# The output product of the last two batches as a two-by-two block product with seven products

## The chip, the cores and the metric

The kernel runs on one core of one Trainium2 chip. The metric is device time in microseconds (us). The matrix engine is TensorE (PE in the rows), its weight loads are listed apart (PEld); VectorE is DVE, ScalarE is ACT, SyncE (SP) issues all transfers.

## What is computed

Attention with a soft cap on its scores for four batches of twelve heads, 448 positions of width 64; the heads laid side by side (768 columns) go through a two-layer block: w_in (768 x 2048), a sigmoid gate, w_out (2048 x 768).

```python
scores = scale * np.matmul(q, k.transpose(0, 1, 3, 2))
scores = cap * np.tanh(scores / cap)
scores = scores - np.max(scores, axis=-1, keepdims=True)
attn = np.exp(scores)
attn = attn / (np.sum(attn, axis=-1, keepdims=True) + 1e-09)
x = np.matmul(attn, v)                          # then (batch, seq, heads * 64)
h = x @ w_in
g = h * (1.0 / (1.0 + np.exp(-1.702 * h)))
return g @ w_out
```

## The kernel before

The work is one batch (448 columns) at a time, numbered 0 to 3, and is written transposed: features on the 128 partitions, positions along the free dimension.

*Attention* goes by units of two heads, six units to a batch. From unit 8 on, all of batches 2 and 3, operands are pairs of 16-bit tiles (a rounded part and the rest). A unit makes four groups of scores into the two double banks of `ps_s` (line 494); ScalarE takes the tanh and the exponential and rounds p, VectorE forms the rest of p and adds the exponentials into `ta` for the sums. There are five p tiles (482), four to a unit. Then come the sums (`ps_sm`) and the products with v (`ps_pa`), one bank each. The sums go through DRAM and come back broadcast as `rb` (two tiles, 486); VectorE multiplies, and `xh` and `xl` are written. For each of the six units there is one tile of xh and one of xl (498), which serve all batches in turn: batch 3's can be written only when batch 2's have been read for the last time.

*h* of a batch (`h_unit`, 727) is 16 chunks of 128 features, `fc`: 6 x 3 matmuls of 128 x 448 into one of two banks (`ps_m`, 409), three because both operands are pairs and the product of the two rests is left out. ScalarE takes the tanh, VectorE multiplies, and `gh`, `gl` are written into one buffer (499) that every batch uses. *The output product* (`o_unit`, 743) is six chunks `dc` of 128 rows, each 16 x 3 matmuls into one bank, one evacuation on ScalarE and one transfer out.

*Order.* The main loop (817) lists attention unit by unit and, in between (`slot`, 785, by the amounts in `BUDGET`), steps of `moe_h` and `moe_o` (768, 778), batch after batch. Each step becomes an operation with its inputs, outputs and an estimated cost. `Plan.schedule` (312) then puts the operations of every engine into a fixed order: up to 20 times it plays them forward, each engine taking the operation that can start first (priority decides ties), and backward, for the latest starts that become the next priorities; the shortest order is written out. Tiles of a ring are given out in the order in which they were asked for. The waits between engines follow from the tiles.

At the end `verdict` (849) forms a flag from column sums kept in `fin` (454) and from a few maxima; only if it is set does a general path run as well (352).

Of the kernel before, what the change touches and what calls it, by code (L numbers as in the profile page):

```python
# [28 lines left out]
DEC_ON = ("AV", "AV")  # L29
EV_ON = ("AV", "AV")  # L30
PASSES = 20
IDLE_MIN, IDLE_STEP = 0.5, 0.06


# [59 lines left out]
class Plan:  # L94
# [263 lines left out]
def fast_path(ctx, tc, flag, q, k, qx, kx, v, cap, w_in, w_out, out):  # L358
# [3 lines left out]
    plan = Plan(tc)  # L362
    B, NP, _, S = q.shape
# [3 lines left out]
    P = 128  # L367
    NC = 8
    NCC = DM // P
    NFC = DFF // P  # L370
# [17 lines left out]
    def ring(shape, dt, name, n, pool=sb):  # L388
        return plan.ring([pool.tile(shape, dt, name=f"{name}{i}") for i in range(n)])
# [19 lines left out]
    ps_m = ring([P, 512], F32, "m", 2, ps)  # L409
# [6 lines left out]
    for i, s in enumerate((1.0, QS * QS)):  # L416
        t = sb.tile([P, 1], F32, name=f"tsc{i}")
# [21 lines left out]
    W0, W1 = 512, 384  # L439
    wi_t = [sb.tile([P, NCC, DFF], F16, name=nm) for nm in ("wi_h", "wi_l")]  # L440
    wo_s = sb.tile([P, 4 * NFC * W1], F16, name="wo")
    wo_t = [[wo_s[:, (2 * c + i) * NFC * W1:(2 * c + i + 1) * NFC * W1].rearrange("p (r w) -> p r w", w=W1) for i in range(2)] for c in range(2)]

    wseq = [(0, r, n, c, W0) for c in range(0, DFF, W0) for r, n in (W_FIRST if c == 0 else ((0, 2), (2, 2), (4, 2)))]
    wseq += [(1, r, WO_ROWS[c], c * W1, W1) for c in range(2) for r in range(0, NFC, WO_ROWS[c])]
    pieces = {}
    wi, wo = {}, {}
# [3 lines left out]
        for i in range(n):  # L451
            (wo if m else wi)[r + i, c] = [x[:, i] for x in both]

    fin = sb.tile([P, len([z for z in wseq if z[0]]) + B * NFC], F32, name="fin")
    fins, fcol = columns(fin, 1)


# [28 lines left out]
    rb_r = ring([P, S], F32, "rb", 2)  # L486
    pu_r = ring([P, S], F32, "pu", 2)
# [255 lines left out]
    def o_unit(b, dc):  # L743
# [11 lines left out]
        plan.scaled(ob, po[:, :S], OS, psum=True)  # L755
        plan.dma([(out[dc * P:(dc + 1) * P, b * S:(b + 1) * S], ob)], P * S * 4e-6)

    ready = set()
    last = {}
    pend = []  # L760
    budget = [0.0]

    def need(m, col):

        while done[0] < len(wseq) and (wseq[done[0]][0] < m or (wseq[done[0]][0] == m and wseq[done[0]][3] <= col)):
            decode_w()

    def moe_h(b):
        while b not in ready:
            yield None  # L770
        for fc in range(NFC):
            need(0, fc * P)
            h_unit(b, fc)
            if b == B - 1 and fc == NFC - 1:
                last["g"] = gs[fc][0]
            yield 3.5

    def moe_o(b):
# [271 lines left out]
```

## Time and profile before

| | |
|---|---|
| three timed runs | 631.75, 632.32, 632.40 us; median 632.32 |
| the profiled execution | 631.68 us, span 629.5 us, granted clock 0.998 |
| TensorE busy | 619.0 us, 98% |
| VectorE, ScalarE busy | 385.8 us (61%), 392.9 us (62%) |
| matmuls h <- x, w_in | 1152 |
| matmuls out <- g, w_out | 1152 |

A busy time is the sum of the listed durations with overlap counted once; matmuls are pipelined, so that what one costs in a stream is read from the time of a long run of them and its count. The page cuts the span into 40 slices; each digit is a busy share in tenths:

```profile
PE   7999999999999999999999999999999999999996
DVE  5688998999788866686664376687664113331000
ACT  6999896799699757778647458779647113331000
```

Attention of the last unit ends near slice 31 of 40; behind it lie h and the output product of batch 3.

### The profile page before, as it was taken

Reading aid. Unit: us, or ns where it says so; the run is one execution under the profiler, and the core shown is the slowest. Engines: PE = TensorE matmul, PEld = TensorE weight load, DVE = VectorE, ACT = ScalarE, POOL = GpSimd, SP = SyncE. Lnnn points to the kernel's source line nnn. Section 1 sums busy time; section 2 is a strip of 40 time slices with the busy share of each in tenths; the row PEclk is TensorE's granted clock in tenths of the full one; section 3 lists DMA queues with packets and bytes.
Section 4 is the critical chain, followed back from the end, with each engine's and each line's share of the span. In section 5 each row is a group of like instructions: output and inputs, shape, how many; then the busy total and the mean of one; then the engine's idle time right before and its main releaser. Section 6 shows DMA issues by size and latency. Waiting matters only on the chain.

```text
span 629.5 us, 9528 instructions
## 1 busy us (share of the span) xinstructions
PE 619.0 (98%) x3743; PEld 296.4 (47%) x3743; DVE 385.8 (61%) x684; ACT 392.9 (62%) x536; POOL 0.2 (0%) x4
## 2 busy tenths in 40 slices
PE   7999999999999999999999999999999999999996
PEld 3343344444444445445445545445445555555553
DVE  5688998999788866686664376687664113331000
ACT  6999896799699757778647458779647113331000
POOL 0000000000000000000000000000000000000000
PEclk9999999999999999999999999999999999999999
DMA  8977651541666821211321321200111100000000
GB/s 301 408 231 195 229 179 51 191 133 56 167 164 191 264 90 32 77 46 46 105 101 35 106 73 48 80 13 18 26 38 44 31 30 1 0 1 17 29 16 34
DMA packets 36340, 61.29 MB, mean 97 GB/s; under 512 B 13928, under 2 KB 21952, under 8 KB 36288
## 3 DMA queue, kind: packets, MB, share of 16 engines
q1 hardware_dynamic: 36288, 60.61, 30.6%
q8 instruction: 31, 0.51, 0.3%
q14 instruction: 21, 0.17, 0.1%
HBM read 54.93 MB, written 5.66 MB: 96 GB/s over the span
## 4 chain that ended last, share of the span: by engine, by line
PE 93%; ACT 2%; DMA 2%; DVE 1%; issue 1%; SPq 0%; ACTq 0%; DVEq 0%
PE m L198 70%; PE s L198 10%; PE pa L198 9%; PE sm L198 3%; DMA wo<-in_moe_w_in_dram 1%; ACT p L155 1%; ACT t L155 1%; ACT wi_h L179 1%; DMA wo<-in_q_dram 1%; ACT wo L179 0%; DVE wi_l L163 0%; DVE wo L163 0%; ACT stg L179 0%; SPq L204 0%; DVE wo L186 0%
## 5 line engine op out<-in xcount | busy, mean ns | idle before, releaser
L198 PE MATMUL m<-gh,wo 128*128 128x448 f16 x768 | 216.2, 353 | 0.0
L198 PEld LDWEIGHTS <-wo 128*128 128x128 f16 x1152 | 110.7, 98 | 107.9 <-issue 7.0
L198 PE MATMUL m<-xh,wi_h 128*128 128x448 f16 x384 | 135.6, 353 | 0.0
L198 PE MATMUL m<-xl,wi_h 128*128 128x448 f16 x384 | 135.4, 353 | 0.0
L198 PE MATMUL m<-gl,wo 128*128 128x448 f16 x384 | 135.4, 353 | 0.0
L198 PE MATMUL m<-xh,wi_l 128*128 128x448 f16 x384 | 135.4, 352 | 0.0
L155 ACT ACTIVATE t<-s,tsc 128x896 f32<-128x896 f32 x96 | 87.0, 907 | 46.5 <-PE s L198 46.4
L198 PEld LDWEIGHTS <-wi_h 128*128 128x128 f16 x768 | 72.8, 98 | 78.7 <-issue 13.7
L163 DVE SCALAR_TENSOR_TENSOR f<-f,m 128x448 f32<-128x448 f32 x64 | 39.5, 618 | 53.1 <-ACT f L155 52.9
L155 ACT ACTIVATE f<-m 128x448 f32<-128x448 f32 x64 | 34.6, 541 | 59.0 <-PE m L198 57.8
L179 ACT ACTIVATE f<-m 128x448 f32<-128x448 f32 x23 | 12.4, 539 | 84.0 <-PE m L198 75.8
L163 DVE TENSOR_TENSOR ta<-ta,t 128x896 f32<-128x896 f32 (+1 forms) x48 | 41.0, 855 | 32.1 <-ACT t L155 30.9
L198 PEld LDWEIGHTS <-wi_l 128*128 128x128 f16 x384 | 37.6, 98 | 35.1
L163 DVE SCALAR_TENSOR_TENSOR wo<-wo 128x1024 int32<-128x1024 int32 (+3 forms) x50 | 51.9, 1053 | 3.2 <-ACT wo L179 2.6
L155 ACT ACTIVATE t<-t,lnb,capt 128x896 f32<-128x896 f32 (+1 forms) x52 | 52.9, 1016 | 1.4
L163 DVE SCALAR_TENSOR_TENSOR gl<-f,gh 128x448 f16<-128x448 f32 x64 | 39.6, 622 | 16.9 <-ACT gh L179 16.3
L163 DVE TENSOR_TENSOR p<-t,p 128x896 f16<-128x896 f32 (+1 forms) x52 | 48.9, 942 | 1.2 <-ACT p L179 0.9
L198 PE MATMUL s<-qh,kk 128*128 128x448 f16 (+3 forms) x160 | 47.5, 401 | 0.0
L179 ACT ACTIVATE p<-t 128x896 f16<-128x896 f32 (+1 forms) x52 | 43.4, 834 | 1.4
L198 PE MATMUL s<-ql,kk 128*128 128x448 f16 (+1 forms) x128 | 39.5, 352 | 0.0
L179 ACT ACTIVATE gh<-f 128x448 f16<-128x448 f32 x51 | 29.1, 570 | 13.7 <-DVE f L163 13.7
L198 PE MATMUL pa<-p,vh 128*64 128x448 f16 x256 | 35.4, 357 | 0.0
(94 smaller groups left out, 545.6 us busy)
## 6 DMA issues: line engine op xcount, KB each, us to landing
wo<-in_moe_w_in_dram SPq DMA_DIRECT2D x24, 512.0 KB
stg<-in_kx_dram SPq DMA_DIRECT2D x16, 448.0 KB
stg<-in_qx_dram SPq DMA_DIRECT2D x16, 448.0 KB
stg<-in_moe_w_out_dram SPq DMA_DIRECT2D x16, 384.0 KB
wo<-in_moe_w_out_dram SPq DMA_DIRECT2D x16, 384.0 KB
out_dram<-f SPq DMA_DIRECT2D x24, 224.0 KB
rb<-rd SPq DMA_DIRECT2D x44, 112.0 KB
vd<-in_v_dram SPq DMA_DIRECT2D x18, 256.0 KB
```

The costliest lines, as they stand in the source:

```text
L155: self.nc.scalar.activation(real(out), real(in_), func, scale=real(scale), **b)
L163: getattr(self.nc.vector, name)(out=real(out), **{k: real(x) for k, x in ins.items()}, **kw, **a)
L179: self.nc.scalar.activation(real(out), real(in_), AF.Copy, scale=1.0 if f is None else f, **b)
L198: self.nc.tensor.matmul(real(o), real(w), real(x), start=a, stop=z)
```

## The change

The output product of batches 2 and 3 together is read as one product of two-by-two blocks. The blocks of w_out are halves of the 2048 features (`j`, 8 chunks each) by halves of the 768 outputs (`i`, three chunks each); the blocks of g are halves of the features by batch. Winograd's form of Strassen's product needs four sums T of blocks of g, four of w_out, seven block products and a few additions behind them. For each of three pairs `d` of output chunks (`d` and `d + 3`) there are seven products of 8 x 3 matmuls, in place of 4 x 16 x 3.

- `difference` replaces the upper right block of w_out by the difference of the upper two, for eight rows, listed after batch 1's output product.
- `h_pair` computes batch 3's h for two chunks, i and i + 8, at a time, and never writes batch 3's g: it forms T1 to T3 and two more operands (`tw`), each split into a pair of 16-bit tiles, from both batches' g. They go to tiles that attention has done with, `tw` to columns of w_in that have been used, in four rows of 112 columns. Its banks are all six of `ps_m` and `ps_s`, and it waits until those are done with.
- `seven_first` (two products, and batch 2's first outputs) runs for d = 0 behind batch 2's h, listed within batch 3's attention; for d = 1, 2 behind batch 3's h.
- `seven_rest` (five products, three outputs) follows; `seven_a` forms three sums of w_out's blocks for a d beforehand, in the space of x and of w_in.
- The x tiles become slices of one tile; `fin` has other columns; the verdict is listed at the end.

```diff
+SPLIT_ON = "A"
+EARLY_FIRST = 1
...
-    x_r = [tuple(ring([P, S], F16, f"{nm}{p}_", 1) for nm in ("xh", "xl")) for p in range(NP)]
+    x_s = sb.tile([P, 2 * NP * S], F16, name="x")
+    x_r = [tuple(plan.ring([x_s[:, (2 * p + i) * S:(2 * p + i + 1) * S]]) for i in range(2)) for p in range(NP)]
...
+    tw = {(k, i): [plan.fixed(t[:, 0:4, (i + k * HF) * P:(i + k * HF) * P + QW]) for t in wi_t] for k in range(2) for i in range(HF)}
...
+    z_r = plan.ring([*ps_m["tiles"], *(t[:, i] for t in ps_s["tiles"] for i in range(2))])
+    e_r = plan.ring([*rb_r["tiles"], *pu_r["tiles"], *f_r["tiles"]])
...
+    def split_to(hi, lo, x, f=1.0, deps=((), ()), judge=False):
+        at(list(deps[0]), plan.scaled, hi, x, None if f == 1.0 else f, on=SPLIT_ON)
+        at(list(deps[1]), plan.stt, lo, x, f, hi, ALU.mult, ALU.subtract, accum_out=fcol() if judge else None)
+
+    def h_pair(i):
...
+        for fc in (i, i + HF):
+            ph = plan.turn(z_r)
...
+            plan.after = after(ps_m, ps_s)
...
+            t = plan.turn(e_r)
+            at(after(rb_r, pu_r, f_r), plan.act, t, ph[:, :S], AF.Tanh, scale=0.851 / HS)
+            plan.stt(t, t, 1.0, ph[:, :S], ALU.add, ALU.mult)
...
+        at(after(rb_r, pu_r, f_r), plan.stt, a, t1, GS, gs[i][0], ALU.mult, ALU.subtract)
+        plan.tt(a, a, gs[i][1], ALU.subtract)
+        tsplit(1, a)
+        plan.tt(t1, t2, t1, ALU.subtract)
+        tsplit(3, t1, GS)
+        split_to(*tw[1, i], four(t2), GS)
+        plan.stt(t2, t2, GS, a, ALU.mult, ALU.subtract)
+        tsplit(2, t2)
+        plan.tt(t2, t2, gs[HF + i][0], ALU.subtract)
+        plan.tt(t2, t2, gs[HF + i][1], ALU.subtract)
+        split_to(*tw[0, i], four(t2))
...
+    def difference(r):
...
+        u = plan.turn(pu_r)[:, :W1]
+        plan.tt(u, a, c, ALU.subtract)
+        plan.tt(u, u, al, ALU.add)
+        plan.tt(u, u, cl, ALU.subtract)
+        split_to(c, cl, u, judge=True)
+
+    def seven_a(d):
...
+        at(first + [x.buf for r in range(HF) for x in wo[r, W1]], plan.tt, u, q[1, 1][0], q[1, 0][0], ALU.subtract)
+        plan.tt(u, u, q[1, 1][1], ALU.add)
+        plan.tt(u, u, q[1, 0][1], ALU.subtract)
+        put(1, u)
+        at(first, plan.tt, w, u, q[0, 0][0], ALU.add)
+        plan.tt(w, w, q[0, 0][1], ALU.add)
+        put(0, w)
+        plan.tt(u, q[0, 1][0], u, ALU.subtract)
+        plan.tt(u, u, q[0, 1][1], ALU.add)
+        put(2, u)
...
+    def seven_first(d):
...
+        late = B - 1 in done_h
+        b1 = bank() if late else plan.turn(ps_m)
+        yield from product(b1, own(0, 0, d), gs[:HF])
+        part[d] = plan.turn(stg)[:, :S]
+        plan.scaled(part[d], b1[:, :S], OS, psum=True)
...
+    def seven_rest(d):
...
+        yield from product(p4, own(1, 1, d), [tw[0, r] for r in range(HF)])
+        seven_a(d)
...
+        yield from product(p7, own(1, 0, d), t_of(3))
...
+        yield from product(p6, s_of(1), t_of(2))
+        plan.stt(u2, p6[:, :S], OS, u2, ALU.mult, ALU.add)
...
+        yield from product(p5, s_of(0), t_of(1))
...
+        yield from product(p3, s_of(2), [tw[1, r] for r in range(HF)])
...
+    def moe_end():
+        while B - 1 not in ready:
+            yield None
+        for i in range(HF):
+            h_pair(i)
+            done_h.add(B - 1)
+            yield 7.0
+        yield from moe_last(range(EARLY_FIRST, HC))
+        for d in range(HC):
+            for _ in seven_rest(d):
+                yield 2.27
...
-            pend.append(moe_h(b))
-            pend.append(moe_o(b))
+            if b < B - 1:
+                pend.append(moe_h(b))
+                if b == B - 3:
+                    pend.append(moe_o(b))
+                    pend.append(moe_s3())
+                else:
+                    pend.append(moe_o(b) if b < B - 2 else moe_last(range(EARLY_FIRST)))
+            else:
+                pend.append(moe_end())
```

## Rows read from the trace of the kernel before

**Rows 1.** Page, part 1: busy time, share of span, instructions of each engine.

```profile
PE 619.0 (98%) x3743; PEld 296.4 (47%) x3743; DVE 385.8 (61%) x684; ACT 392.9 (62%) x536; POOL 0.2 (0%) x4
```

**Rows 2.** Windows, us: time, PE, PEld, DVE, ACT, POOL busy (count), clock, DMA, GB/s.

```profile
375.50:442.00 66.50, 66.50 (x388) 33.10 (x387) 47.81 (x86) 50.87 (x68) 0.00 (x0) 1.00 0.15 48
442.00:494.00 52.00, 52.00 (x326) 25.60 (x324) 27.46 (x42) 28.99 (x39) 0.00 (x0) 1.00 0.13 33
...
515.00:570.00 55.00, 55.00 (x293) 28.44 (x291) 19.38 (x46) 17.33 (x31) 0.00 (x0) 1.00 0.01 5
570.00:623.40 53.40, 53.40 (x284) 27.45 (x282) 1.62 (x9) 3.37 (x7) 0.00 (x0) 1.00 0.06 22
```

**Rows 3.** Chain of work that ended last, after 493 us: start, us, what.

```profile
493.74 129.50 PE m L198 x684
```

**Rows 4.** Groups by shape, whole run: engine operation shapes xcount | busy us, mean ns | idle.

```profile
L198 PE MATMUL m<-gh,wo 128*128 128x448 f16 x768 | 216.2, 353 | 0.0
...
L163 DVE SCALAR_TENSOR_TENSOR gl<-f,gh 128x448 f16<-128x448 f32 x64 | 39.6, 622 | 16.9 <-ACT gh L179 16.3
L163 DVE SCALAR_TENSOR_TENSOR f<-f,m 128x448 f32<-128x448 f32 x64 | 39.5, 618 | 53.1 <-ACT f L155 52.9
...
L179 ACT ACTIVATE gh<-f 128x448 f16<-128x448 f32 x51 | 29.1, 570 | 13.7 <-DVE f L163 13.7
...
L163 DVE SCALAR_TENSOR_TENSOR wi_l<-wo,wi_h 128x1024 f16<-128x1024 f32 x11 | 13.4, 1218 | 1.8 <-ACT wi_h L179 1.8
...
L163 DVE SCALAR_TENSOR_TENSOR wo<-stg,wo 128x384 f16<-128x384 f32 x16 | 8.8, 553 | 1.2 <-ACT wo L179 1.2
```

**Rows 5.** DVE timeline, three operations in a row: start, us, operation.

```profile
443.11 0.63 DVE L163 SCALAR_TENSOR_TENSOR xl<-rb,xh 128x448 f16<-128x448 f32 x1
443.65 0.61 DVE L163 SCALAR_TENSOR_TENSOR f<-f,m 128x448 f32<-128x448 f32 x1
444.19 0.62 DVE L163 SCALAR_TENSOR_TENSOR xl<-rb,xh 128x448 f16<-128x448 f32 x1
```

**Rows 6.** ACT timeline from the end of batch 2's h: start, us, operation.

```profile
442.12 0.56 ACT L179 ACTIVATE xh<-rb 128x448 f16<-128x448 f32 x1
...
445.64 0.53 ACT L155 ACTIVATE f<-m 128x448 f32<-128x448 f32 x1
...
448.59 1.01 ACT L155 ACTIVATE t<-s,tsc 128x896 f32<-128x896 f32 x1 [1.15 <-PE s L198]
449.63 1.13 ACT L155 ACTIVATE ta<-t,lnb,capt 128x896 f32<-128x896 f32 x1
450.79 0.95 ACT L179 ACTIVATE p<-ta 128x896 f16<-128x896 f32 x1
...
462.47 0.62 ACT L155 ACTIVATE t<-s,tsc 128x448 f32<-128x448 f32 x1
463.12 0.76 ACT L155 ACTIVATE t<-t,lnb,capt 128x448 f32<-128x448 f32 x1
463.91 0.58 ACT L179 ACTIVATE p<-t 128x448 f16<-128x448 f32 x1
```

**Rows 7.** Timeline of all engines around the last attention unit's end.

```profile
486.66 0.62 ACT L155 ACTIVATE t<-s,tsc 128x448 f32<-128x448 f32 x1
...
490.76 0.59 PE L198 MATMUL sm<-ta,ones 128*32 128x224 f32 x8
...
502.48 0.62 DVE L163 TENSOR_TENSOR rb<-pa,rb 128x448 f32<-128x448 f32 x1 [6.82 <-DMA rb<-rd]
...
505.23 0.54 ACT L179 ACTIVATE f<-m 128x448 f32<-128x448 f32 x1 [8.54 <-PE m L198]
...
505.67 0.57 ACT L179 ACTIVATE xh<-rb 128x448 f16<-128x448 f32 x1
...
506.28 0.62 DVE L163 SCALAR_TENSOR_TENSOR xl<-rb,xh 128x448 f16<-128x448 f32 x1 [3.18 <-ACT xh L179]
```

**Rows 8.** Windows again: the stretch after the last matmul (clock is third last).

```profile
626.00:629.50 3.50, 0.00 (x0) 0.00 (x0) 0.00 (x0) 0.00 (x0) 0.00 (x0) 0.70 0.04 12
```

More of the change, by code (lines that the diff above doesn't have):

```diff
@@ L452, in fast_path @@
             (wo if m else wi)[r + i, c] = [x[:, i] for x in both]
-    fin = sb.tile([P, len([z for z in wseq if z[0]]) + B * NFC], F32, name="fin")
+    fin = sb.tile([P, len([z for z in wseq if z[0]]) + (B - 1) * NFC + 2 + NFC // 2 + 3 * NCC // 2], F32, name="fin")
     fins, fcol = columns(fin, 1)
@@ L756, in o_unit, with after, blocks, flat16 @@
         plan.dma([(out[dc * P:(dc + 1) * P, b * S:(b + 1) * S], ob)], P * S * 4e-6)
+    HF, HC = NFC // 2, NCC // 2
+    QW = S // 4
+    def after(*rings):
+        return [b for r in rings for b in r["turns"]]
+    def blocks(t, n):
+        return [t[:, i * S:(i + 1) * S] for i in range(n)]
+    def flat16(t):
+        return t.rearrange("p a s -> p (a s)").bitcast(F16)
+    room_t = [(x, p_r) for t in p_t for x in blocks(t.rearrange("p w i s -> p (w i s)"), 4)]
+    room_t += [(x, r) for r in (t_r, ta_r) for t in r["tiles"] for x in blocks(flat16(t), 4)]
@@ new lines, in fast_path @@
+    room_t += [(x, r) for r in rings.values() for t in r["tiles"] for x in blocks(t.rearrange("p a s -> p (a s)"), 2)]
+    room_t += [(t[:, S:].bitcast(F16)[:, :S], stg) for t in stg_t]
+    t_at = {(k, i, w): (plan.fixed(x), r) for (k, i, w), (x, r) in zip(((k, i, w) for k in (1, 2, 3) for i in range(HF) for w in range(2)), room_t)}
+    tw = {(k, i): [plan.fixed(t[:, 0:4, (i + k * HF) * P:(i + k * HF) * P + QW]) for t in wi_t] for k in range(2) for i in range(HF)}
+    sw = {k: [plan.fixed(t[:, NCC - 2 + k // 2, k % 2 * HF * P:(k % 2 + 1) * HF * P].rearrange("p (r w) -> p r w", w=P)) for t in wi_t] for k in range(3)}
@@ new lines, in fast_path, with at @@
+    us = [plan.fixed(x_s[:, i * 2 * HF * P:(i + 1) * 2 * HF * P].bitcast(F32).rearrange("p (r w) -> p r w", w=P)) for i in range(2)]
+    z_r = plan.ring([*ps_m["tiles"], *(t[:, i] for t in ps_s["tiles"] for i in range(2))])
+    e_r = plan.ring([*rb_r["tiles"], *pu_r["tiles"], *f_r["tiles"]])
+    part = {}
+    done_h = set()
+    def at(deps, f, *a, **k):
+        plan.after = deps
+        f(*a, **k)
+        plan.after = []
+    def split_to(hi, lo, x, f=1.0, deps=((), ()), judge=False):
+        at(list(deps[0]), plan.scaled, hi, x, None if f == 1.0 else f, on=SPLIT_ON)
+        at(list(deps[1]), plan.stt, lo, x, f, hi, ALU.mult, ALU.subtract, accum_out=fcol() if judge else None)
@@ new lines, in quad, with put @@
+    def quad(i, j, d):
+        return [wo_t[i][w][:, j * HF:(j + 1) * HF, d * P:(d + 1) * P] for w in range(2)]
+    def difference(r):
+        (a, al), (c, cl) = wo[r, 0], wo[r, W1]
+        u = plan.turn(pu_r)[:, :W1]
[4 more added lines that the diff above has]
+    def seven_a(d):
+        q = {(i, j): [plan.fixed(x) for x in quad(i, j, d)] for i in range(2) for j in range(2)}
+        u, w = us
+        first = after(*(r for rs in x_r for r in rs)) if d == 0 else []
+        free = [x.buf for v in pieces.values() for x in v] if d == 0 else []
+        def put(k, x):
+            split_to(*sw[k], x, deps=(free, free), judge=True)
+        at(first + [x.buf for r in range(HF) for x in wo[r, W1]], plan.tt, u, q[1, 1][0], q[1, 0][0], ALU.subtract)
[8 more added lines that the diff above has]
+        put(2, u)
@@ new lines, in product @@
+    def product(out, lhs, mov):
+        for r in range(HF):
+            (wh, wl), (gh, gl) = lhs[r], mov[r]
+            o = out[:, :S]
+            if len(gh.shape) == 3:
+                o = o.rearrange("p (a w) -> p a w", w=QW)
+            plan.mm(3 * FULL, "full", [
+                (o, a, x, r == 0 and w == 0, r == HF - 1 and w == 2) for w, (a, x) in enumerate(((wh, gh), (wh, gl), (wl, gh)))
+            ])
+            plan.after = []
+            if r % 4 == 3 and r < HF - 1:
+                yield
@@ new lines, in own, with send, bank @@
+    def own(i, j, d):
+        return [[x[:, d * P:(d + 1) * P] for x in wo[j * HF + r, i * W1]] for r in range(HF)]
+    def send(ob, i, b, d):
+        dc = i * HC + d
+        plan.dma([(out[dc * P:(dc + 1) * P, b * S:(b + 1) * S], ob)], P * S * 4e-6)
+    def bank():
+        plan.after = after(ps_m, ps_s)
+        return plan.turn(z_r)
+    def seven_first(d):
[4 more added lines that the diff above has]
+        plan.scaled(part[d], b1[:, :S], OS, psum=True)
+        yield
+        b2 = bank() if late else plan.turn(ps_m)
+        yield from product(b2, own(0, 1, d), gs[HF:])
+        ob = plan.turn(e_r if late else f_r)
+        at(after(rb_r, pu_r, f_r) if late else [], plan.stt, ob, b2[:, :S], OS, part[d], ALU.mult, ALU.add)
+        send(ob, 0, B - 2, d)
@@ L773, in moe_h, with moe_s3, moe_last @@
             h_unit(b, fc)
-            if b == B - 1 and fc == NFC - 1:
-                last["g"] = gs[fc][0]
             yield 3.5
+    def moe_s3():
+        for r in range(HF):
+            difference(r)
+            yield 0.5
+    def moe_last(ds):
+        for d in ds:
+            for _ in seven_first(d):
+                yield 2.27
+            yield 2.27
+    def moe_end():
[8 more added lines that the diff above has]
+            for _ in seven_rest(d):
+                yield 2.27
+            yield 2.27
+            if d == HC - 1:
+                last["g"] = gs[NFC - 1][0]
     def moe_o(b):
```

45 lines of the change are left out of this document (added).

## The prediction

> **What bounds the kernel now.** I read the page's engine line first: TensorE is busy in 98% of the span, VectorE and ScalarE in 61% and 62% [rows 1]. The windows then show that this is an average over stages that differ: while batch 2's h runs, VectorE is busy 47.8 and ScalarE 50.9 of 66.5 us; in the stage of batch 3's h 19.4 and 17.3 of 55 us; in the last stage 1.6 and 3.4 of 53.4 us; TensorE fills all of them [rows 2]. So TensorE's amount of work sets the time now, and the other two have room at the end but much less where attention runs. The chain of waits says the same: its last long piece is one run of 684 matmuls in 129.50 us, 0.1893 us for each [rows 3]. Those are h of batch 3 (16 x 18 = 288), the output product of batch 3 (6 x 48 = 288) and 108 left over from batch 2's output product. The listed mean of 353 ns [rows 4] is a matmul's time through a pipeline, not its cost in a stream.
>
> **What is removed.** The output products of batches 2 and 3 are 2 x 6 x 16 x 3 = 576 matmuls. The change does seven block products for each of three column pairs, 7 x 8 x 3 x 3 = 504. 72 matmuls x 0.1893 = 13.6 us [rows 3]. All of these lie on the path. The profiled run took 631.68 us, 2.18 of it outside the span of 629.5 and 0.64 under the median of the three timed runs; without any loss the change would give 631.68 - 13.63 = 618.05.
>
> **What moves: the filler of the last attention.** Batch 2's output product is not only work; it covers. Of its 288 matmuls 180 (34.1 us) run while the last attention units wait on ScalarE and VectorE, and 108 (20.4 us) while the last unit's sums make their way through DRAM [rows 3]. In the new order only two of the seven products of the first column pair (48 matmuls, 9.1 us) can run there; the others need batch 3's g. The place begins where batch 2's h ends, since the x tiles have one buffer: the first two units of batch 3 get their xh written only at 442.12 and after, when the last h unit stops reading, and that unit's tanh starts at 445.64 [rows 6], so its last matmul ended near 445.6. From there to 493.74 TensorE worked 48.1 us, 34.1 of them filler, so attention's own share is 14.0 us, 3.0 of it the last unit's sums and products (490.76 to 493.74) [rows 3, 7]. In the new order it has 14.0 - 3.0 + 9.1 = 20.1 us of work until the scores of the last unit are evacuated (the h matmuls of batch 3 wait for all score banks). If the last tanh of the last unit starts by 445.6 + 20.1 = 465.7, nothing is lost; before, it starts at 486.66 [rows 7]. Every us beyond 465.7 is a us of idle TensorE.
>
> How early can it be? Unit 4's first tanh starts at 448.59. A unit's ScalarE work is three groups of 1.01 + 1.13 + 0.95 and one of 0.62 + 0.76 + 0.58, 11.2 us [rows 6]. Unit 4 whole, unit 5 without its last exponential and cast (11.2 - 1.34 = 9.9) and up to four short casts and evacuations of some 0.56 each, 2.2, make 23.3: the last tanh at 448.6 + 23.3 = 471.9 if ScalarE never waits and nothing goes to VectorE. Lower end: half of the casts go to VectorE (3.5 us less) and unit 4 starts when its keys allow, so 465.7 or earlier, loss 0. Upper end: the pace of before, in which unit 4 took 448.59 to 462.47 from first to last tanh [rows 6], 13.9 us, twice with a 2.5 us gap: 448.6 + 13.9 + 2.5 + 13.9 = 478.9, loss 13.2; with the very times of before 486.66, loss 21.0. I take 471.9, loss 6.2 us, since ScalarE's own rows carry it.
>
> After that tanh, sums, DRAM, product, xh and xl take until 506.90, 20.2 us, 2.5 of which xh stands behind an evacuation on ScalarE that waits for TensorE (rb is ready at 503.10, xh starts at 505.67) [rows 7]; so 17.7 to 20.2. TensorE has 3.0 us of that unit and, now that six banks may hold h, six units of 15 matmuls that don't need the last x: 90 x 0.1893 = 17.0. Together 20.0, so nothing more is lost there. Last x: 471.9 + 17.7 = 489.6.
>
> **What is added, and where it hides.** *Batch 3's h.* For each pair of fc VectorE has 13 operations of 128x448 in place of 4, ScalarE 6 in place of 4; TensorE needs 36 x 0.1893 = 6.8 us for a pair. VectorE's listed time is 0.62 [rows 4], but three such operations in a row start 0.54 apart [rows 5]: 13 x 0.54 = 7.0 us a pair, 56.2 for eight. ScalarE, 6 x 0.57 = 3.4, is covered. *The weight sums* of a column pair: seven subtractions or additions and three splits of 128x1024, at 1.22 listed and so 1.14 in a row (estimate: the same 0.08 less) [rows 4, 5]: 11.4 us of VectorE for each 22.7 us of TensorE (120 matmuls), hidden for the second and third pair, with six evacuations of 0.62 beside it. *The difference of w_out's halves*: 8 x 4 operations of 128x384 at 0.55 [rows 4], 17.7 us, wanted only after batch 3's h; VectorE is idle in 47% of the 52 us after batch 2's h [rows 2] and again while the last sums are under way, so I cost it at nothing. From the last x at 489.6, VectorE needs 56.2 + 11.4 + 1.1 (two evacuations), 68.7 us, until the last weight sum of the first column pair, and then TensorE has one product of that pair and two whole pairs, 264 matmuls or 50.0 us. That path ends at 608.3; TensorE's own at 623.24 - 13.63 + 6.2 = 615.8. So TensorE still carries the end, with 7.5 us to spare.
>
> The Trainium skill speaks against that cover: "VectorE: DVE Perf Modes", section "The DRAIN you can't avoid", has it that the next VectorE instruction does not start until the pipeline of the one before is empty. Here it starts 0.08 us before the listed end [rows 5], so the trace does not bear it out in full; taken at the listed 0.62 and 1.22 the sum would be 64.5 + 12.2 + 1.2 = 77.9 us, the path would end at 617.5 and the run 1.7 us later.
>
> *The moving operand in pieces.* Two of the seven products read T as four runs of 112 columns, a form that no row has. I take the price of the plain matmul; the upper end is the listed 353 ns for each of 2 x 72 matmuls [rows 4], 144 x 0.164 = 23.6 us; a gain is excluded, as the columns are the same number. *Queues*: SyncE issues the same 24 output transfers. The first part sum takes one of the four staging tiles through which keys and queries come; a load behind it would be late by one product, 24 x 0.1893 = 4.5 us, which belongs to A. *The end*: one VectorE operation in place of one ScalarE evacuation, under 0.1 us. *Small bubbles* where work of three engines is now tied closer: 1.0 us, between 0 and 4.
>
> Sum: 631.68 - 13.63 + 6.2 + 1.0 = 625.25.
>
> **Rivals.** A, the slower side: attention after batch 2's h does not speed up, because its pace was set by its own waits (score banks, one bank for the products, five p tiles) and not by the filler. Then the gain is eaten: the point is a last tanh at 465.7 + 13.6 = 479.3. With the times of before it is 618.05 + 21.0 + 1 = 640; with unit 5 right behind unit 4 at the old pace 618.05 + 13.2 + 1 = 632.3. For it: unit 4's first two groups lie 5.5 us apart where their ScalarE work is 3.1. Against it: VectorE and ScalarE are busy only 53% and 56% there [rows 2].
>
> B: VectorE becomes the bound in batch 3's h. It decides once VectorE has 7.5 us more than my 68.7. With listed durations it gives 627; with the 17.7 us of differences put off until there as well, 618.05 + 7.2 + 1.7 + 17.7 = 645. Half of that, some 635, is its middle.
>
> C: no loss at all, the attention is fast enough: 618 to 620.
>
> D: the clock. After the last matmul the granted clock is 0.70 over the last 3.5 us [rows 8], so it falls from 2.4 to 1.2 GHz when TensorE has stopped. The idle time that I forecast lies in pieces of a us or so between scores and products, so I leave it at nothing; in one piece it would slow the matmuls behind it. The Trainium skill, "TensorE: Matmul & The Clock Gate", section "Why this matters for your kernels", warns of such gaps between bursts; the trace agrees as far as its last stretch shows.
>
> E: the change does not do what it says: the flag sends the run into the general path as well, or the pieces of T cost as above (640).
>
> **How the numbers follow.** My forecast (620 to 630) 0.52, C 0.15, A 0.17 (half of it about 632, half slower), B 0.12 (a third of it under 630), D and E 0.04. Faster than 632.32 by over 0.2%, which is about what a measurement of this kernel can tell from no change (under 631.05): 0.52 + 0.15 + 0.04 = 0.71. Within: 0.09. Slower, over 633.6: 0.20, the rest of A and B, D and E. The range of 8 in 10 reaches from 618.0 (C) to 634.5, which takes in A's nearer end and the middle of B. Time: 625.3.
>
> **What would show it.** The matmuls of the output products should number 1080 in place of 1152. Right, if TensorE is idle for some 4 to 8 us between 445 and 472, in small pieces that wait for scores or p, and dense from there on; if the last unit's last tanh starts at 468 to 476; if in batch 3's h VectorE is busy over 85% and TensorE doesn't wait for it. Wrong, if TensorE waits on tiles written in batch 3's h (B), if its gaps lie in one piece with a lower clock (D), if matmuls on T's pieces start more than 0.19 us apart (E), or if the last tanh starts after 479 (A).

## The result and the profile after

The changed kernel takes 622.52 us (median of four runs, 621.96 to 623.3) where the kernel before took 632.36 in the same session (631.75 to 633.11): a ratio of 0.9845, 95% interval 0.9828 to 0.9862. That is 9.8 us less; the forecast was 625.3 with a range of 618.0 to 634.5. The time lies between the forecast and rival C. The profiled run took 622.88 us, 2.2 of them outside its span of 620.7, as before.

The page's engine line, in the form of [rows 1]:

```profile
PE 607.4 (98%) x3679; PEld 288.4 (46%) x3679; DVE 487.8 (79%) x845; ACT 408.6 (66%) x565; POOL 0.2 (0%) x4
```

VectorE has 102.0 us more to do than in [rows 1], ScalarE 15.7 more, and TensorE 11.6 less. Of TensorE's 3679 matmuls 85 are the small ones that the kernel puts into idle time at its start; before there were 77 of those among 3743. The rest went from 3666 to 3594, exactly the 72 that the change promises.

The windows (time, then busy time and count of PE, PEld, DVE, ACT and POOL, the granted clock, the DMA share, GB/s) for two of the stretches of [rows 2]:

```profile
375.50:442.00 66.50, 66.50 (x392) 31.84 (x387) 59.66 (x116) 52.55 (x74) 0.00 (x0) 1.00 0.14 42
515.00:570.00 55.00, 53.65 (x284) 27.58 (x282) 48.31 (x75) 17.76 (x30) 0.00 (x0) 1.00 0.03 9
```

TensorE is still full in the first. In the second it misses 1.35 us, and VectorE went from 19.4 us of the 55 to 48.3; in the 21 us ahead of it, from 494 to 515, VectorE is busy 20.7. So in batch 3's h VectorE now has hardly more room than TensorE. The chain of waits (start, us, what), where [rows 3] had one piece of 129.50 us:

```profile
429.86 3.41 PE m L200 x18
433.27 0.50 PE s L200 x4
433.77 3.51 PE m L200 x18
...
468.53 4.65 PE m L200 x24
473.17 3.41 PE s L200 x18
...
518.80 11.93 PE s L200 x63
530.75 0.55 ACT stg L181
531.35 8.67 PE s L200 x45
...
549.67 10.80 PE s L200 x57
560.49 0.64 DVE rb L165
561.17 6.97 PE s L200 x36
...
604.46 9.10 PE m L200 x48
613.58 0.62 DVE rb L165
```

It is still a chain of TensorE, with two short stops (an evacuation on ScalarE at 530.75, one on VectorE at 560.49). Where did the gain go? The span is 8.8 us shorter, the removed matmuls are worth 13.63, so 4.83 us are lost, and nearly all of them can be placed:

- 0.55 us up to the end of batch 2's h: of the matmuls on wi_l the 277th of 384, close to that end, starts at 438.86 and started at 438.31 (the order of the earlier stages changed a little). Six matmuls on v, some 0.6 us, that stood ahead of this point before now stand behind it.
- 1.35 us in the two stops, as idle time is listed, from the listed end of one matmul. From start to start they cost 1.68: the matmuls behind them start 0.99 and 1.07 us after the ones ahead, in place of 0.19.
- 0.88 us behind the last matmul: the span ended 6.26 us after it and now ends 7.14 after it.
- 2.05 us is what remains. 0.3 of it is the rest of the two stops, 0.6 the six matmuls on v, and 0.9 changes of the stationary tile's shape, which is listed ahead of the operand's size:

```profile
448.52 0.55 PE L200 MATMUL m<-x,wi_h 128*128 128x448 f16 x2
448.90 0.35 PE L200 MATMUL m<-x,wi_l 128*128 128x448 f16 x1
449.19 0.38 PE L200 MATMUL s<-qh,kk 128*64 128x448 f16 x2
```

A matmul ahead of such a change takes 0.28 to 0.29 us to the next start, where others of 128x448 take 0.19; so 18 matmuls behind a change take 3.51 us in the chain where others take 3.41. From the end of batch 2's h to the last matmul the changed kernel has 25 such changes and the kernel before 15: ten more at 0.094 us. All ten lie in the last attention; behind 494 us the chain goes from `m` to `s` and back without a change of shape, and 72 matmuls take 13.62 us as before. Some 0.2 us are left that no row explains.

How the attention's end came out (ScalarE's timeline: start, us, operation, and in brackets the idle time before it and what ended it):

```profile
441.88 1.01 ACT L157 ACTIVATE t<-s,tsc 128x896 f32<-128x896 f32 x1 [0.42 <-PE s L200]
...
461.50 0.62 ACT L157 ACTIVATE t<-s,tsc 128x448 f32<-128x448 f32 x1
...
479.67 0.58 ACT L181 ACTIVATE x<-rb 128x448 f16<-128x448 f32 x1 [6.89 <-DVE rb L165]
```

These answer to 448.59 of [rows 6] and to 486.66 and 505.67 of [rows 7]: unit 4 starts 6.7 us earlier than before, the last tanh of the last unit comes 25.2 us earlier, the last x 26.0. What stood ahead of unit 4's scores on TensorE, before (two lines) and after (two lines; the last is the end of batch 2's h):

```profile
447.44 0.35 PE L198 MATMUL m<-gh,wo 128*128 128x448 f16 x1
447.63 0.35 PE L198 MATMUL s<-qh,kk 128*128 128x448 f16 x1
...
440.91 0.36 PE L200 MATMUL s<-qh,kk 128*128 128x448 f16 x1
...
450.64 0.35 PE L200 MATMUL m<-x,wi_l 128*128 128x448 f16 x1
```

Before, the scores came behind all of batch 2's h and behind 12 matmuls of filler. After, they come ahead of the last 30 matmuls of batch 2's h.

### The profile page after: what moved, and what is told of

The parts are those of the page before. It is cut to its first block, busy times and chain, and to the rows that moved or that the text cites. A ratio compares the mean times of both kernels' runs of the same rounds, so it can differ in the third digit from the quotient of the medians.

```text
span 620.7 us, 9566 instructions
## 1 busy us (share of the span) xinstructions
PE 607.4 (98%) x3679; PEld 288.4 (46%) x3679; DVE 487.8 (79%) x845; ACT 408.6 (66%) x565; POOL 0.2 (0%) x4
## 4 chain that ended last, share of the span: by engine, by line
PE 93%; DMA 2%; DVE 2%; ACT 1%; issue 0%; SPq 0%; DVEq 0%; ACTq 0%
PE m L200 54%; PE s L200 26%; PE pa L200 10%; PE sm L200 4%; DVE wo L165 1%; DMA rb<-rd 1%; DMA rd<-rr 1%; DMA wo<-in_q_dram 1%; DVE wi_l L165 0%; ACT wo L181 0%; ACT t L157 0%; ACT p L157 0%; DVE rb L165 0%; SPq L206 0%; ACT wi_h L181 0%
## 5 line engine op out<-in xcount | busy, mean ns | idle before, releaser
L200 PE MATMUL m<-x,wi_h 128*128 128x448 f16 x648 | 175.8, 353 | 0.0
L200 PEld LDWEIGHTS <-wi_h 128*128 128x128 f16 x912 | 86.4, 98 | 93.4 <-issue 16.5
L200 PE MATMUL m<-gh,wo 128*128 128x448 f16 x432 | 124.4, 353 | 0.0
L200 PEld LDWEIGHTS <-wo 128*128 128x128 f16 x864 | 82.5, 98 | 82.7 <-issue 8.5
L200 PE MATMUL m<-x,wi_l 128*128 128x448 f16 x324 | 114.2, 352 | 0.0
L200 PE MATMUL m<-gl,wo 128*128 128x448 f16 x216 | 76.1, 352 | 0.0
L157 ACT ACTIVATE f<-m 128x448 f32<-128x448 f32 x49 | 26.4, 539 | 26.0 <-PE m L200 25.5
L165 DVE SCALAR_TENSOR_TENSOR gl<-f,gh 128x448 f16<-128x448 f32 x48 | 29.6, 622 | 4.6 <-ACT gh L181 4.0
L200 PE MATMUL s<-x,wi_h 128*128 128x448 f16 x120 | 32.5, 353 | 0.0
L200 PEld LDWEIGHTS <-kk 128*128 128x128 f16 (+1 forms) x256 | 20.5, 100 | 24.7 <-issue 8.4
```

Of the source, the lines that this page charges most:

```text
L157: self.nc.scalar.activation(real(out), real(in_), func, scale=real(scale), **b)
L165: getattr(self.nc.vector, name)(out=real(out), **{k: real(x) for k, x in ins.items()}, **kw, **a)
L200: self.nc.tensor.matmul(real(o), real(w), real(x), start=a, stop=z)
```

## The experiments

"Changed kernel" is the kernel of the diff; each experiment edits it, except one that edits the kernel before. Times are medians; a ratio is against the kernel before in the same session, with its 95% interval.

### 1. One product more in each column pair

```diff
         yield from product(p7, own(1, 0, d), t_of(3))
         yield
+        yield from product(p7, own(1, 0, d), t_of(3))
+        yield
         p6 = bank()
```

> The changed kernel with the eighth product given back: in each of the three column pairs the product of T3 is done twice in the same bank, the first time for nothing, 72 matmuls more. If TensorE carries the time through the last stages, it costs 72 x 0.1893 = 13.6 us, less what falls into TensorE's few waits: 634.5 to 636.5, slower than before by 0.4 to 0.6%. If VectorE bound batch 3's h and the stage behind it, much of the extra work would lie in TensorE's waits: 630 or less.

Measured: 637.55 us, ratio 1.0083 (1.0068 to 1.0098), 15.0 us over the changed kernel and 1 us past the range expected. The 72 matmuls cost all of their 13.6 us, and somewhat more than that: TensorE's waits for evacuations grew from 1.35 to 3.5 us, it may be because a bank stays taken longer; no run isolates that. So TensorE's work is on the path, one for one; nothing behind it absorbs a product. With seven plus one products the scheme is slower than the old eight.

### 2. No filler left beside the last attention

```diff
-EARLY_FIRST = 1
+EARLY_FIRST = 0
```

> EARLY_FIRST = 0: all of the seven-product scheme waits for batch 3's h, so 48 matmuls (9.1 us) leave the stretch of the last attention and the same number comes later. Theory: attention is now as fast as ScalarE allows, and what TensorE has there is what covers it; after the last score group TensorE had some 3 us of work beyond the arrival of the last x, so 9.1 - 3.4 = 5.7 us become idle: 627 to 629, with gaps of TensorE between 440 and 485. Rival: the last chunks of batch 2's h are spread wide enough to cover it: under 624.

Measured: 630.26 us, ratio 0.9969 (0.9956 to 0.9982), 7.7 us over the changed kernel and past both expectations. The filler's 9.1 us are worth most of their length there. TensorE's own rows in the place, and two windows, from the profiled run (631.95 us):

```profile
463.35 0.35 PE L200 MATMUL m<-x,wi_l 128*128 128x448 f16 x1
466.51 1.45 PE L200 MATMUL sm<-ta,ones 128*32 128x224 f32 x8 [2.82 <-DVE ta L165]
467.89 0.93 PE L200 MATMUL m<-x,wi_h 128*128 128x448 f16 x2
```

```profile
464.00:468.00 4.00, 1.40 (x9) 0.40 (x10) 3.83 (x7) 2.31 (x4) 0.00 (x0) 0.92 0.03 1
468.00:471.20 3.20, 3.20 (x10) 1.27 (x10) 2.58 (x6) 0.36 (x1) 0.00 (x0) 0.56 0.29 78
```

TensorE waits 2.82 us for VectorE's sum of ta, and then its matmuls start 0.37 us apart, not 0.19: the granted clock of the second window is 0.56 of full speed, so it has fallen from the higher of its two levels (2.4 GHz) to the lower (1.2) for most of it. By 471.2 it is back at 1.00. The chain has 3.22 us for nine matmuls that are 1.70 at full clock, so the fall cost 1.5 us in these nine. That is rival D's mechanism: it is not in the trace of the changed kernel, and it is there when the filler is gone. The rest is 2.7 us of waits for ScalarE at 454 and 456, the 2.82, and another 1.4 us of waits for evacuations in the last stage.

### 3. Two pairs of filler there

```diff
-EARLY_FIRST = 1
+EARLY_FIRST = 2
```

> Two column pairs of batch 2's first products (96 matmuls, 18.2 us) lie beside the last attention units, in place of one (48, 9.1 us). Theory: with one pair TensorE no longer waits there, so more filler buys nothing: 622 to 623.5 us. First rival: the bubbles of the stretch 440 to 494 come from work that is too thin, and more of it closes them: 620.5 to 621.5. Second rival: the filler stands in front of the last units' scores and moves the last x behind 484: over 625.

Measured: 625.72 us, ratio 0.9899 (0.9884 to 0.9914), 3.2 us over the changed kernel. The second rival's time, but only a part of its reason: the last x came 2.8 us later (483.05, where it was 480.28), and VectorE started batch 3's h at 488.20 in place of 484.29; but in experiment 5 it started at 489.05 and nothing was lost. TensorE has no gap at the last x. It waits later, from 490 on (engine, line, what it waited for, us in total, times, longest):

```profile
PE m L200 <- DVE stg L165: 0.9, 1, 0.9
PE s L200 <- DVE stg L165: 0.7, 1, 0.7
PE s L200 <- ACT pu L157: 0.6, 1, 0.6
PE s L200 <- ACT f L157: 0.6, 1, 0.6
PE s L200 <- ACT stg L181: 0.6, 1, 0.6
PE s L200 <- DVE wi_l L165: 0.3, 1, 0.3
```

3.9 us in all before rounding, where the changed kernel has 1.35. The 48 matmuls that moved forward had stood between batch 3's h and the products that need T and the weight sums. By this reading they gave VectorE the time to finish both there, and now its results are late (stg holds pieces of T, wi_l the weight sums). So the filler is wanted in two places, and one pair here, two pairs there is the best of the three splits run (none, one and two pairs here): 630.3, 622.5, 625.7.

### 4. The last two chunks of batch 2's h in one piece

```diff
...
+            if b == B - 2 and fc >= NFC - 2:
+                whole += part_mm
+            else:
+                plan.mm(3 * FULL, "full", part_mm)
+        if whole:
+            plan.mm(3 * NCC * FULL, "full", whole)
```

> The last two chunks of batch 2's h can no longer be cut: each is one operation of 18 matmuls instead of six of three. If the loss foreseen at the end of attention did not come because these two chunks were spent three matmuls at a time between the attention groups, while the x tiles came free one by one, then TensorE now waits there: 625 to 629. If only the total of the work counts and not its cutting: 623.5 or less.

Measured: 623.15 us, ratio 0.9853 (0.9838 to 0.9868). The rival held: the time is within 0.7 us of the changed kernel's. But the cutting does matter for when unit 4 starts. ScalarE's row:

```profile
446.52 1.01 ACT L157 ACTIVATE t<-s,tsc 128x896 f32<-128x896 f32 x1 [0.15 <-PE s L200]
```

Here the scores stand right behind the last h matmul, with no filler between: 2.1 us earlier than before (448.59) and 4.6 later than in the changed kernel (441.88), where they stand among the parts of the last h units. The last tanh came at 466.16, 0.5 us past the break-even point of the prediction, and TensorE waited 1.0 us for the sum of ta. So the early start of the changed kernel has some 4 us more than it needs.

### 5. Another price for VectorE in the plan, in both kernels

```diff
-    "dve": (0.155, 0.00104), "dve2": (0.14, 0.00056), ...
+    "dve": (0.075, 0.00104), "dve2": (0.06, 0.00056), ...
```

> The plan's cost of a VectorE operation is 0.08 us less (0.54 for 448 columns, as three in a row show, in place of 0.62); nothing else changes, but the order of all engines is planned anew. If TensorE's two waits of some 0.9 us in the last stage (an evacuation queued on ScalarE ahead of splits that were ready, six banks all taken) come from a plan that takes VectorE for slower than it is, they go: 620.5 to 622. If they come from the banks as such: 622 to 624.

Measured: 621.97 us, ratio 0.9833 (0.9819 to 0.9846); not to be told from the changed kernel, and at the border of the two expectations. A wait for the evacuation on ScalarE is still there, 1.5 us long. This run did not settle what causes it.

The same edit in the kernel before:

> The kernel before, with eight block products, whose plan enters VectorE operations 0.08 us shorter; nothing else is changed, so only the order of the work differs. It tells how far another order alone moves the time where TensorE fills every stage. Theory: the old kernel has room everywhere, so another order moves it by less than 1 us: 631.5 to 633 us. Rival: an order from the plan is worth several us in either kernel, and what the changed kernel gained could in part be the luck of its order: under 630 or over 635 us.

Measured: 633.36 us, ratio 1.002 (1.0009 to 1.0031). Another order alone moves the old kernel by 1.3 us (by the ratio) the wrong way, a little past the 633 expected. Two orders of the old kernel lie at 632.4 and 633.4, two of the changed kernel at 622.5 and 622.0: by these the gain is not an order's luck. That an order can cost several us all the same is seen in experiment 7.

### 6. The first part sums evacuated by VectorE

```diff
-        plan.scaled(part[d], b1[:, :S], OS, psum=True)
+        plan.scaled(part[d], b1[:, :S], OS, on="V", psum=True)
```

> The first part sum of each column pair is evacuated by VectorE alone; ScalarE takes it now and waits for TensorE with splits of T queued behind it. Theory: the wait of TensorE at 530.7 goes (0.6 to 0.8 us): 621.5 to 622 us, and in the trace no wait of TensorE on a staging tile. Rival: the wait only changes its engine, since the banks are taken in turn: 622 to 623 us with as long a wait elsewhere.

What it is meant for, in the changed kernel (ScalarE, then VectorE):

```profile
530.75 0.54 ACT L181 ACTIVATE stg<-s 128x448 f32<-128x448 f32 x1 [5.82 <-PE s L200]
531.19 0.57 ACT L181 ACTIVATE t<-rb 128x448 f16<-128x448 f32 x1
```

```profile
526.92 0.61 DVE L165 SCALAR_TENSOR_TENSOR f<-f,m 128x448 f32<-128x448 f32 x1
531.79 0.62 DVE L165 SCALAR_TENSOR_TENSOR t<-rb,t 128x448 f16<-128x448 f32 x1 [4.26 <-ACT t L181]
```

ScalarE stands 5.82 us in front of an evacuation that TensorE has not finished; the split of T behind it in ScalarE's queue reads what VectorE had finished by 527.5, and VectorE, which needs that split, stands 4.26 us. Measured: 622.23 us, ratio 0.9841 (0.9828 to 0.9855). The wait on ScalarE is gone, and there is one of 0.7 us for the staging tile on VectorE in its place, beside the old one at rb. The rival held: the wait changed its engine. VectorE's pause of 4.26 us is gone too, here and in experiment 5, and neither run is faster by more than can be measured: by these runs the pause costs the changed kernel nothing.

### 7. Experiments 5 and 6 together

> Two small edits together: VectorE operations entered 0.08 us shorter in the plan that orders the work, and the first part sums evacuated by VectorE. Theory: each moves a wait of TensorE without removing it, so together they are within what can be measured: 621.5 to 622.5 us. Rival: together they close the waits of 0.6 to 0.8 us in the last stage: 620 to 621.2 us.

Measured: 626.58 us, ratio 0.9923 (0.9904 to 0.9941): neither; two edits that alone were worth nothing cost 4.1 us together. In the last stage TensorE waits 5.5 us (2.6 for rb, 2.1 for staging tiles, 0.7 for f), 4.1 more than in the changed kernel, which is the whole difference. In the chain ahead of its longest wait there is only VectorE, without a pause from 540 to 553.9; its end:

```profile
552.22 1.14 DVE wi_l L165 x2
553.36 0.55 DVE rb L165
553.91 0.04 issue
553.95 7.55 PE s L200 x39
```

VectorE's weight sums (operations on x from 544.5 on, wi_l at 552.22) stand ahead of the evacuation into rb for which TensorE waits. That is rival B in the small: VectorE has so little room that the order of its queue decides over several us. The granted clock stays at 1.00 behind this wait of 2.6 us.

### 8. All high halves of the splits on VectorE

```diff
-SPLIT_ON = "A"
+SPLIT_ON = "V"
```

> The high halves of the splits in batch 3's h and in the weight sums go to VectorE, not ScalarE: 5 operations of 128x448 a pair, listed at 0.39 us on VectorE and so some 0.31 in a row, are 12.4 us for eight pairs, and three of 128x1024 at 0.61 are 1.8 us: VectorE has 14.2 us more to do between the last x and the last weight sum of the first column pair. Theory (the sum of the prediction with the last x where it is now, 480.3): 480.3 + 68.7 + 14.2 + 50.0 = 613.2, as late as TensorE's own end of 613.6, so VectorE just keeps up: 622 to 626 us. Rival (VectorE works at its listed durations, 77.9 us, and is at its limit already): 480.3 + 77.9 + 14.2 + 50.0 = 622.4, 8.8 us later: 629 to 635 us.

Measured: 641.22 us, ratio 1.0149 (1.0133 to 1.0164), 18.7 us over the changed kernel: beyond both. My price for the added work was too low. A pair of h took 10.15 us of VectorE (the first operations of successive pairs start at 492.96, 503.11, 513.26) where the changed kernel took 7.32 (497.10, 504.42, 511.75): 2.83 us more, where 5 x 0.31 = 1.55 was expected. The rows say why (VectorE's timeline):

```profile
484.53 0.62 DVE L165 TENSOR_TENSOR pu<-pu,gl 128x448 f32<-128x448 f32 x1
485.19 0.39 DVE L186 CAST p<-pu 128x448 f16<-128x448 f32 x1
485.61 0.63 DVE L165 SCALAR_TENSOR_TENSOR p<-pu,p 128x448 f16<-128x448 f32 x1
486.15 0.62 DVE L165 TENSOR_TENSOR rb<-rb,rb 128x448 f32<-128x448 f32 x1
```

The cast of pu, which reads what the operation ahead of it wrote, starts 0.66 us after it, and the low half that reads the cast 0.42 after a cast listed at 0.39. The operation at 486.15, which needs nothing from the one ahead, starts 0.54 after it. So a step costs 0.54 if it is independent of the one before and 0.66 if it is not, and a split on VectorE adds a cast that waits for its input and a low half that waits for the cast. Eight pairs are 22.6 us more VectorE work. Two windows of 10 us show what that does (TensorE's busy time first, VectorE's third, the clock third last):

```profile
510.00:520.00 10.00, 7.72 (x33) 3.54 (x32) 9.52 (x18) 1.09 (x2) 0.00 (x0) 0.83 0.01 2
530.00:540.00 10.00, 6.82 (x29) 3.02 (x27) 9.48 (x19) 0.00 (x0) 0.00 (x0) 0.83 0.00 0
```

VectorE is full, TensorE waits, and the clock falls behind its waits here too: after one of 2.28 us it is 0.51 from 514 to 517.

### 9. Two of the five on VectorE

```diff
...
-        split_to(*tw[1, i], four(t2), GS)
+        split_to(*tw[1, i], four(t2), GS, on="V")
...
-        split_to(*tw[0, i], four(t2))
+        split_to(*tw[0, i], four(t2), on="V")
```

> Of the five splits of a pair in batch 3's h two (the pieces of T) have their high half on VectorE. With all five there a pair took 10.15 us, not 7.32, 0.57 for each, so two are 1.13 us a pair and 9.1 us in eight pairs. In the changed kernel the last weight sum of the first column pair ends at 562.25, and with the 50.0 us of TensorE work behind it that path ends at 612.2, 1.3 us ahead of TensorE's own end. Theory (1.3 us of slack): 7.8 us later: 629 to 632 us. Rival (the 7.5 us to spare that were forecast are there): 1.6 us later: 623 to 625 us.

Measured: 627.73 us, ratio 0.994 (0.9918 to 0.9962), 5.2 us over the changed kernel, between the two. A pair takes 8.30 us (498.19, 506.50, 514.79), so 0.98 more, 7.8 us in eight pairs. At 552 TensorE waits 2.7 us for a piece of T in a staging tile, and behind that the granted clock is 0.66 from 555 to 560: 11 matmuls take 3.77 us from 555.10, in place of 2.08, so 1.7 us are the clock's. VectorE's pause of 4.26 us shrank to 1.73, and the path over the last weight sum had the 1.3 us in hand that the expectation names: 7.8 - 2.5 - 1.3 + 1.7 = 5.7, near the 5.2 lost. So VectorE has some 4 us of room in this stage by this run, neither 1.3 nor 7.5. In experiment 8, 18.7 us were lost of 22.6 added in h and some 2 in the first weight sums, so 6 cost nothing; what the clock took there is not set apart.

### 10. Shorter weight sums

```diff
         at(first + ..., plan.tt, u, q[1, 1][0], q[1, 0][0], ALU.subtract)
-        plan.tt(u, u, q[1, 1][1], ALU.add)
-        plan.tt(u, u, q[1, 0][1], ALU.subtract)
         put(1, u)
         at(first, plan.tt, w, u, q[0, 0][0], ALU.add)
-        plan.tt(w, w, q[0, 0][1], ALU.add)
         put(0, w)
         plan.tt(u, q[0, 1][0], u, ALU.subtract)
-        plan.tt(u, u, q[0, 1][1], ALU.add)
```

> The four corrections by low halves are left out of each column pair's weight sums, so the last bits of three of the seven products are not computed: three operations of 128x1024 in place of seven, some 4.7 us less VectorE work ahead of the first weight sums and 14 us in all. Theory: TensorE carries the end and VectorE only keeps up, so little is gained, at most the waits of the last stage: 621 to 622.5 us. Rival: VectorE's work in batch 3's h and the weight sums is what sets the end by now, and all of the 4.7 us come back: 617 to 619 us.

Measured: 631.17 us, ratio 0.9975 (0.9958 to 0.9993): 8.6 us slower, outside both. The total says nothing on the question, since the plan found another order for the whole kernel. Already the 13th of the matmuls on wi_l starts 5.2 us later than in the changed kernel (92.48, not 87.27), the 37th 9.2, and the 97th, near the start of batch 1's h, 9.9; TensorE waits 3.3 us for one tile in that start (1.6 in the changed kernel), fills idle time with 170 small matmuls, not 85, and from 60 to 70 us its granted clock is 0.78, not 1.00. The stretch in question can be read all the same: from the first matmul on batch 3's x tiles (477.43 and 468.53) to the last matmul of all it takes 145.9 us, and 145.0 in the changed kernel. Three operations in place of seven gave nothing back there, so by this reading VectorE's weight sums were not on the path; TensorE carried it.

### 11. Two banks for batch 3's h

```diff
+    zh_r = plan.ring(ps_m["tiles"])
...
-            ph = plan.turn(z_r)
+            ph = plan.turn(zh_r)
...
-        plan.after = after(ps_m, ps_s)
+        plan.after = after(ps_m, ps_s, zh_r)
```

> Batch 3's h may use two PSUM banks, not six, so two units of 15 matmuls (5.7 us) can be worked on before the last x, in place of six (17.0 us). Theory: the six banks cover the time in which the last unit's sums go through DRAM; without four of them 11.3 us of cover are gone and TensorE stands still in one piece: 629 to 634 us, more if the granted clock falls behind the gap. Rival: the last x comes early enough for the cover to be spare: 622 to 625 us.

Measured: 625.46 us, ratio 0.9886 (0.9869 to 0.9902), 2.9 us over the changed kernel, 0.5 past the rival's range and far from the theory's. TensorE's waits around the last x (its timeline):

```profile
477.28 0.35 PE L200 MATMUL m<-x,wi_h 128*128 128x448 f16 x1 [0.46 <-ACT x L181]
...
479.83 0.54 PE L200 MATMUL m<-x,wi_h 128*128 128x448 f16 x2 [0.78 <-DVE rb L165]
```

Between 460 and 480 TensorE misses 1.55 us, not 11.3; 0.7 more comes in the last stage, where it waits three times for an evacuation. Four of six banks were nearly spare at this place. The changed kernel itself puts only 48 of the 90 partial matmuls ahead of the last x (24, 18 and 6 in its chain up to 480.2), and with them it holds that x up: its last unit's product starts at 476.51, behind 42 of them, and here at 470.85, behind 12. So here the last x is there at 477.26, 3 us sooner, and needs that much less cover.

## Why the prediction was right or wrong

**72 matmuls, 13.6 us.** Right, in their count (3594 for 3666) and in their price (experiment 1).

**The filler, 6.2 us: the step that failed.** Its mechanism was right: there is a break-even for the last tanh. With less cover TensorE stops (experiment 2), and at 466.16 it loses about a us (experiment 4); the longest stops there end at VectorE's sum of ta, which follows that tanh, and not at ScalarE. The size was wrong: the last tanh came at 461.50, before 465.7, not at 471.9, and TensorE had no idle time between 445 and 472, where 4 to 8 us were the sign of being right; the loss was 0 and not 6.2. 6.7 us of this are unit 4's start. I took its first tanh from the old trace, 448.59 [rows 6], as though ScalarE could not start it earlier, though the same row shows that ScalarE waited for scores from TensorE. In the new order it is 441.88. The old filler ahead of those scores is only the smaller part: without it, and with the scores still behind batch 2's h, unit 4 starts at 446.52 (experiment 4). The other 4.6 us come from scores that stand ahead of the last 30 matmuls of batch 2's h, which I had not thought of: not only the filler but the end of h can cover the attention. The remaining 3.7 us are the pace: two units took 19.6 us and not 23.3, in part because casts went to VectorE (one at 448.25), as my lower end had it. My lower end named the cause ("unit 4 starts when its keys allow") and I did not take it.

**Sums and last x.** The time from the last tanh to the last x, 17.7 to 20.2 us, was right: 461.50 to 480.91, the end of xl, is 19.4. That it would cost nothing was right too, but my reason was only a part of it: the six banks, 17.0 us of cover, could shrink to two for 1.55 us of TensorE's time there (experiment 11).

**Batch 3's h and the weight sums on VectorE.** The conclusion was right, TensorE carries the end (experiments 1 and 10), but the 7.5 us to spare were not. By my own sum the earlier last x would have raised them to 480.3 + 68.7 + 50.0 = 599.0 against TensorE's 613.6, so 14.6 us; experiment 9 found some 4, and in experiment 8 no more than 6 cost nothing. Three terms were too small. A pair takes 7.32 us, not 7.0, since some of the 13 steps depend on the one ahead: 2.6 us. VectorE starts only at 484.29, when TensorE has finished the first unit, 4.0 us behind the last x. And it pauses 4.26 and 1.76 us behind ScalarE's and TensorE's evacuations. With these 12.6 us the sum comes to 561.6 for the last weight sum of the first column pair; it ended at 562.25. ScalarE has seven operations for a pair (two tanh, five high halves), not the six that I counted; at 0.57 they are 4.0 us and covered. The Trainium skill, "VectorE: DVE Perf Modes", section "The DRAIN you can't avoid", has it that the next VectorE operation does not start until the pipeline of the one before is empty. The trace agrees where an operation reads what the one before wrote (0.66 us for 0.62 listed), which is nearer than I let it; where it does not depend on the one before, the trace shows 0.54.

**Differences at no cost.** Right in the price, not in the place: they run on VectorE between 215 and 427 us, ahead of the stretches that I named, and TensorE misses nothing in any window between 75 and 500.

**T in pieces.** Right: the last product of the first column pair reads T as four runs of 112 columns, and its 24 matmuls take 4.54 us from 563.43, 0.189 each. Rival E is out.

**The end.** Under 0.1 us was forecast; 0.88 measured. Behind the last matmul there is now an evacuation of 0.62 us on VectorE, and the flag's chain stands behind it in VectorE's queue (613.58 to 614.20), where before it started 0.19 us behind the last matmul. That makes the flag some 0.4 us later. The other 0.5 lies behind the flag's last operation (5.9 us to the end of the span, and 5.4 before), and no row explains it.

**Small bubbles.** 1.0 us (0 to 4) was forecast. 3.95 were measured: 1.7 of stops for evacuations, 0.9 of changes of shape, 1.1 early in the kernel (0.55 late with six matmuls fewer done), 0.2 that is not placed. The changes of shape had no term in the sum.

Together: 631.68 - 13.63 + 0 + 3.95 + 0.88 = 622.88, the profiled run. The forecast was 2.4 us above it because 6.2 us that did not come outweighed 3.8 us of small terms that came on top. That it was so near is in part luck: two errors of opposite sign.

**Rivals.** A is out: attention sped up by 25 us. C describes the attention and not the time, since it left the small terms out. B is not what happened, but near: experiments 7, 8 and 9 show TensorE waiting for VectorE as soon as VectorE has some us more, or another order. D did not happen, as the clock is 1.00 in every window from 375 to 600, but experiments 2, 8 and 9 show it. The Trainium skill, "TensorE: Matmul & The Clock Gate", section "Why this matters for your kernels", warns of idle gaps between bursts of matmuls. The trace of experiment 2 agrees, with 1.5 us behind a wait of 2.82 us; behind the 2.6 us of experiment 7 the clock stayed.

What stays open: 0.2 us in the stages and 0.5 at the end have no row that explains them, and no run changes the number of changes of shape alone. Which order would close the two stops of 0.6 and 0.7 us was not found; three tries moved them or made them worse. No version run beats the changed kernel by more than can be measured (621.97 and 622.23 against 622.52).

## What to carry to other kernels

When a change takes away the work that covered a wait, ask first whether the old start of the covered stage was itself set by the order of the engine that gave the cover; a row whose idle time ends at that engine says so, and the work of the stage before may cover as well. When the bounding engine's work is cut and another engine gets a hundred us more, look at how much room that engine has in the one stage where its results are wanted, counting dependent steps at their full length and its queue's pauses. Here the order of its queue cost 4 us (experiment 7) where its sum still fitted. Filler is worth most where it stands between a producer and its consumer, and there can be two such places: split it by trying, as in experiments 2 and 3.

## What was not expected of the hardware

- On VectorE an operation on 128x448 starts 0.54 us after an independent one and 0.66 us after one on which it depends (both listed at 0.62). It depends also if it only overwrites what the one ahead still reads. From 485 to 575 us of experiment 8, 62 of 99 such neighbours lie 0.65 or 0.66 apart: in 46 the second reads the tile that the first wrote, in 16 it writes the tile that the first read. The other 37 lie 0.53 or 0.54 apart; in four of them a tile's name is the same, with buffer numbers left out.
- TensorE's clock fell to its lower level behind a single wait of 2.82 us (experiment 2) and was back at 1.00 by 471.2, 4.7 us after the wait's end; matmuls started 0.37 us apart in between. It fell behind a wait of 2.28 us in experiment 8 too, and stayed at 1.00 behind one of 2.60 us in experiment 7: the length of the wait alone does not tell.
- A change of the stationary tile's shape costs TensorE 0.09 us: 0.28 to 0.29 us from start to start and not 0.19.
